# Lightning attention feeding a two-layer MLP on one core: every transpose of k, q and x' moved from the DMA queue to TensorE, and one more group of layer 2 computed as seven block products

## The chip, the cores and the metric

The kernel runs on one core of one Trainium2 chip. The metric is the device time of one execution in microseconds (us). It is given as the median of several executions, and one further view of the work comes from a single execution that the hardware profiler recorded. Engines are called PE (TensorE), DVE (VectorE), ACT (ScalarE), POOL (GpSimd) and SP (SyncE, which here only issues DMAs); PEld is the weight load of TensorE, which the profile lists apart from the matmuls.

## The reference, cut to what matters

Inputs are q, k, v of shape (4 batches, 8 heads, 768 positions, 64), one decay factor per head, a normalization weight of 512 and two weight matrices of 512 x 2048 and 2048 x 512.

```python
for b in range(nb):                       # blocks of 64 positions
    intra = einsum('bhic,bhjc->bhij', qb, kb) * Dmask       # Dmask = lam^(i-j), lower triangle
    intra = einsum('bhij,bhjd->bhid', intra, vb)
    inter = einsum('bhid,bhde->bhie', qb * lam_pow, kv_state)
    out[:, :, sl] = intra + inter
    kv_state = lam_block * kv_state + einsum('bhsd,bhse->bhde', kb * rev_pow, vb)
# x = out, heads side by side: (4, 768, 512)
xn = (x - mean(x)) / sqrt(var(x) + 1e-6) * g_ln
y  = x + relu(xn @ w_ch1) @ w_ch2
```

## The kernel before, in words

The 3072 rows of x are cut into twelve **windows** u of 256 positions of one batch. Each window goes through an attention part and then, as **group** g = u of two tiles of 128 rows, through the MLP.

The attention part of a window loads k, q and v (`load_in`, lines 76 and 80), scales and casts them to bf16 on POOL, DVE or ACT (`in_k_one`, `in_q_one`, `in_v`; lines 231, 236, 242), and needs k and q transposed, so that the head dimension lies on the partitions. The transposed pair is the tile `kqT`. With it the scores (line 279 in the early windows, 370 later) are multiplied on PE, masked on DVE (289, 376), multiplied with v (`av`, lines 436 and 423), and the part that comes from the running state is added (`inter`, line 449). Between the two halves of `inter` stands a fence, `reader` (line 460): a small copy of the PSUM bank, on ACT for most windows, which PE has to wait for. `norm` (lines 475 to 477) takes the row sums on ACT and writes x', the row minus its mean times the weight, as bf16 `xc` on DVE. The reciprocal standard deviation, `rstd_of` (lines 520 to 525), is applied only after layer 2.

x' must be transposed too (`to_xT`, lines 494 to 511), because layer 1 contracts over the 512 features. Layer 1 of a group is eight steps on PE: each is one PSUM bank, filled by eight matmuls with 256 columns (line 547), or, where a chunk is taken tile by tile, by sixteen with 128 columns (line 658), and emptied by ACT with a ReLU into fp16 `hT` (lines 550, 661). Layer 2 has two forms. Groups 0 to 3 use sixteen plain matmuls with 512 columns per tile (line 684, evicted at 708). Groups from `WG = 4` on use a scheme of **seven block products** in place of eight (`product`, line 582; each is eight matmuls with 256 columns): it needs sums of blocks of `hT` (`h_sums`, lines 565 to 567, DVE), sums of blocks of the weights (`w_sums`, lines 809 to 813, DVE, once), and a longer eviction (`evict`, lines 595 to 615, on ACT, POOL and DVE).

The transposes are done in two ways. `transpose_pe` (line 250, copied at 251) serves the first three windows: PE multiplies by an identity, the result lies in PSUM, and ACT or DVE copies it out. From window 3 on, `transpose_dma` (line 257) and `transpose_both` (line 263) let SP issue a DMA transpose from SBUF to SBUF. `to_xT` uses PE and an ACT copy for windows 0 to 4 (lines 510, 511) and a DMA transpose for windows 5 to 11 (line 503).

The order of the work is written out by hand, from line 1043 to the end. `plan` lists the layer steps of all groups, sixteen for each group from 2 on, and `units(n)` emits the next n of them. Between them stand the attention pieces: `s12`, `Y(u)` and `X(u)` interleave window u's scores with window u - 1's output, and loads, casts, transposes and stores each have their place. Every engine takes its own instructions in the emitted order. PSUM has a pool of four banks `mm` (layer 1, layer 2, `kv`, the early scores), two banks `sc` (scores) and one each of `po0` and `po1` (attention output).

Of the kernel before, what the change touches and what calls it, by code (L numbers as in the profile page):

```python
# [8 lines left out]
BF16 = mybir.dt.bfloat16  # L9
# [8 lines left out]
def kernel(  # L18
# [11 lines left out]
    nc = tc.nc  # L30
# [5 lines left out]
    DM = H * D  # L36
    DF = moe_w_ch1.shape[1]
    NP = H // 2
# [5 lines left out]
    XS = 64.0  # L44
    WG = 4
    assert D == 64 and S % W == 0 and DM == 512
# [11 lines left out]
    XB = 3  # L58
    X_PE = (2, 3, 4)
    LB = 6  # L60
# [191 lines left out]

    def transpose_dma(u, a):
        s = st[u]
        if "kqT" not in s:
            s["kqT"] = wk.tile([128, 2, NP, 2, 128], BF16, tag="kqT", bufs=3, name="kqT")
        nc.sync.dma_start_transpose(s["kqT"][:, a].rearrange("p b j t -> p (b j) t"),
                                    s["kq"][:, a].rearrange("p b j e d -> p (b j e d)"))

    def transpose_both(u):  # L260
        s = st[u]
        s["kqT"] = wk.tile([128, 2, NP, 2, 128], BF16, tag="kqT", bufs=3, name="kqT")
        nc.sync.dma_start_transpose(s["kqT"].rearrange("p a b j t -> p (a b j) t"),
                                    s["kq"].rearrange("p a b j e d -> p (a b j e d)"))

# [189 lines left out]
    def reader(u, act=False):  # L455
        s = st[u]
        for ab in range(2):
            if s["S"][ab][1] is not None:
                seen = wk.tile([128, H], F32, tag="seen", name="seen")
                (nc.scalar.copy if act or u > WG else nc.vector.tensor_copy)(seen, s["po"][ab][:, :, 0])  # L460

# [32 lines left out]
    def to_xT(u, ab):  # L494
        s = st[u]
        t = 2 * u + ab
        g = group_of[t]
        i = t - groups[g][0]
        if i == 0:
            xT_of[g] = gp.tile([128, KA, GT * 128], BF16, tag="xT", bufs=3, name="xT")  # L500
        dst = xT_of[g][:, :, i * 128:(i + 1) * 128]
        if u >= 2 and u not in X_PE:
            nc.sync.dma_start_transpose(dst, s["xc"][:, ab])
        else:
            if u < 2:
                xt = mm_tile([128, KA, 128], BF16, "xt")
            else:
                xt = ps.tile([128, KA, 128], BF16, tag=f"po{ab}", name="xt")
            for kk in range(KA):
                nc.tensor.transpose(xt[:, kk, :], s["xc"][:, ab, kk * 128:(kk + 1) * 128], ident)  # L510
            nc.scalar.copy(dst, xt)  # L511

# [19 lines left out]
    def mlp(g):  # L532
# [134 lines left out]
        def m2(i, part):  # L667
# [13 lines left out]
            if part == 0:  # L681
                acc[i] = mm_tile([128, DM], F32, "pm2")
            for kk in range(part * 4, part * 4 + 4):
                nc.tensor.matmul(acc[i], lhsT=hT[:, kk, i * 128:(i + 1) * 128], rhs=w2[kk // W2K][:, kk % W2K, :],  # L684
                                 start=(kk == 0), stop=(kk == KB - 1))
            if part == KB // 4 - 1:
# [251 lines left out]

    def Y(u):
        kv(u)  # L940
        av(u - 1, range(NP))
        inter(u - 1, 0, fence=False)
        reader(u - 1, act=True)
        scores(u, 0)
        scores(u, 1, early=True)
        inter(u - 1, 1)
        new_state(u, 0, nc.gpsimd)
        mask(u, 0, (0,))
        new_state(u, 1, nc.gpsimd)
        norm(u - 1, 0)  # L950
        norm(u - 1, 1)
        mask(u, 1)
        mask(u, 0, (1,))

# [91 lines left out]
    for g in range(2, len(groups)):  # L1046
        m1, m2 = mlp(g)
        lo = {3: 3, 4: 3, 5: 2, 6: 2}.get(g, NWC)
        plan += [(m1, n) for n in range(2 * lo)] + [(m1.tile, c, i) for c in range(lo, NWC) for i in range(2)]
        if g >= WG:  # L1050
            plan += [(m2.w, n) for n in range(8)]
        else:
            plan += [(m2, i, part) for i in range(len(groups[g])) for part in range(KB // 4)]
# [37 lines left out]
    s4(2)  # L1091
    in_k_one(3, nc.vector, 1)
    transpose_dma(3, 0)
    transpose_dma(3, 1)
    load_in(4, "v", nc.sync)
    units(2)
    open_in(5, False)
    load_in(5, "k", nc.sync)
    to_xT(2, 0)
    units(1)  # L1100
    load_in(5, "q", nc.sync)
    rstd_of(2)
# [6 lines left out]
    in_q_one(4, nc.gpsimd, 1)  # L1109
    transpose_dma(4, 0)  # L1110
    transpose_dma(4, 1)
    load_in(5, "v", nc.sync)
# [3 lines left out]
    w_sums(0, 0)  # L1116
    units(2)
    w_sums(0, 1)
    w_sums(1, 0)
    units(3)  # L1120
    s12(3)
    store(0)
    units(3)
    open_window(5)
    in_k_one(5, nc.gpsimd, 0)
    in_k_one(5, nc.gpsimd, 1)
    in_q_one(5, nc.gpsimd, 0)
    in_q_one(5, nc.gpsimd, 1)
    units(2)
    w_sums(1, 1)  # L1130
    open_in(6, False)
    load_in(6, "k", nc.sync)
    units(1)
    load_in(6, "q", nc.sync)
    units(1)
    load_in(6, "v", nc.sync)
    units(1)
    Y(4)
    in_v(5, nc.gpsimd)
    transpose_dma(5, 0)  # L1140
    transpose_dma(5, 1)
    units(3)
    to_xT(3, 0)
    to_xT(3, 1)
    open_in(7, False)
    load_in(7, "k", nc.sync)
    units(1)
    open_window(6)
    in_k_one(6, nc.scalar, 0)
    in_k_one(6, nc.gpsimd, 1)  # L1150
    units(3)
    in_q_one(6, nc.vector, 1)
    in_v(6, nc.gpsimd)
    open_window(7)
    units(1)
    in_q_one(6, nc.vector, 0)
    w_sums(2, 0)
    units(1)
    w_sums(2, 1)
    units(2)  # L1160
    load_in(7, "q", nc.sync)
    w_sums(3, 0)
    units(1)
    rstd_of(3)
    w_sums(3, 1)
    open_in(8, False)
    units(4)
    Y(5)
    transpose_dma(6, 1)
    load_in(7, "v", nc.sync)  # L1170
    units(1)
    in_q_one(7, nc.gpsimd, 0)
    units(1)
    to_xT(4, 0)
    in_q_one(7, nc.gpsimd, 1)
    transpose_dma(6, 0)
    units(1)
    to_xT(4, 1)
    units(1)
    rstd_of(4)  # L1180
    units(2)
    in_k_one(7, nc.vector, 1)
    load_in(8, "k", nc.sync)
    load_in(8, "q", nc.sync)
    in_v(7, nc.gpsimd)
    units(1)
    in_k_one(7, nc.scalar, 0)
    units(1)
    m2s[4].sums(0, 4)
    units(1)  # L1190
    X(6, rest=False)
    open_window(8)
    transpose_dma(7, 0)
    transpose_dma(7, 1)
    to_xT(5, 0)
    to_xT(5, 1)
    store(1)
    store(2)
    units(3)
    m2s[4].sums(4, 8)  # L1200
    mask64(6, 1)
    open_in(9, False)
    units(1)
    units(2)
    in_k_one(8, nc.vector, 1)
    load_in(8, "v", nc.sync)
    load_in(9, "k", nc.sync)
    units(2)
    in_q_one(8, nc.gpsimd, 0)
    in_q_one(8, nc.gpsimd, 1)  # L1210
    in_k_one(8, nc.gpsimd, 0)
    rstd_of(5)
    units(3)
    units(1)
    X(7)
    units(1)
    in_v(8, nc.gpsimd)
    units(1)
    to_xT(6, 0)
    transpose_dma(8, 1)  # L1220
    transpose_dma(8, 0)
    to_xT(6, 1)
    load_in(9, "q", nc.sync)
# [6 lines left out]
    load_in(10, "v", nc.sync)  # L1230
    units(2)
    open_window(9)
    units(1)
    m2s[5].sums(4, 8)
    units(3)
    in_k_one(9, nc.scalar, 0)
    units(1)
    in_k_one(9, nc.scalar, 1)
    units(1)
    rstd_of(6)  # L1240
    X(8)
    in_q_one(9, nc.gpsimd, 0)
    units(1)
    in_q_one(9, nc.gpsimd, 1)
    open_window(10)
    units(3)
    open_in(11, False)
    units(1)
    to_xT(7, 0)
    units(1)  # L1250
    transpose_dma(9, 1)
    transpose_dma(9, 0)
    to_xT(7, 1)
    units(2)
    load_in(10, "q", nc.sync)
    store(3)
    units(2)
    m2s[6].sums(0, 4)
    m2s[6].sums(4, 8)
    units(3)  # L1260
    store(4)
    units(3)
    rstd_of(7)
    units(1)
    in_v(9, nc.gpsimd)
    in_k_one(10, nc.gpsimd, 1)
    in_k_one(10, nc.gpsimd, 0)
    X(9)
    in_v(10, nc.gpsimd)
    in_q_one(10, nc.gpsimd, 0)  # L1270
    units(1)
    transpose_dma(10, 0)
    units(1)
    in_q_one(10, nc.vector, 1)
    units(1)
    to_xT(8, 0)
    units(2)
    to_xT(8, 1)
    units(1)
    transpose_dma(10, 1)  # L1280
    units(3)
    m2s[7].sums(0, 4)
    m2s[7].sums(4, 8)
    units(1)
    load_in(11, "q", nc.sync)
    units(1)
    load_in(11, "k", nc.sync)
    units(2)
    load_in(11, "v", nc.sync)
    units(2)  # L1290
    rstd_of(8)
    units(1)
    X(10)
    units(1)
    to_xT(9, 0)
    to_xT(9, 1)
    open_window(11)
    in_q_one(11, nc.gpsimd, 0)
    in_q_one(11, nc.gpsimd, 1)
    units(1)  # L1300
    in_k_one(11, nc.scalar, 0)
    units(1)
    in_k_one(11, nc.scalar, 1)
    transpose_both(11)
    units(1)
    m2s[8].sums(0, 4)
    units(1)
    in_v(11, nc.gpsimd)
    units(3)
    m2s[8].sums(4, 8)  # L1310
    units(1)
    store(5)
    units(6)
    rstd_of(9)
    units(1)
    X(11)
    units(1)
    to_xT(10, 0)
    to_xT(10, 1)
    units(3)  # L1320
    m2s[9].sums(0, 4)
    units(4)
    m2s[9].sums(4, 8)
    units(7)
    rstd_of(10)
    units(1)
    wind_up(11)
    units(1)
    to_xT(11, 0)
    to_xT(11, 1)  # L1330
    store(6)
# [8 lines left out]
    m2s[10].sums(4, 8)  # L1340
    units(7)
    rstd_of(11)
# [36 lines left out]
```

## Time and profile before

| | |
|---|---|
| median of 7 runs | 207.95 us (206.65 to 208.25) |
| the profiled execution | 206.65 us |
| its span, first to last instruction | 204.9 us |
| PE busy, matmuls | 195.7 us, 96% of the span, x3229 |
| DVE busy | 133.3 us, 65% |
| ACT busy | 122.6 us, 60% |
| POOL busy | 84.7 us, 41% |
| granted TensorE clock, mean | 0.998 |
| DMA transposes issued by SP | 17 for kqT, 14 for xT |

The span is shorter than the execution by 1.75 us; that part lies outside the instructions. In the profile's lines, L250 is line 250 of the kernel. A line of a group gives the engine, the operation, output and input tiles, the shapes, the number of instructions, and then the busy time, the mean duration of one, and the idle time before them. A line of the timeline gives the start, the time covered, the engine and the operation. Matmuls overlap, so the mean duration of one is longer than the distance between two of them; that distance is read from the starts in the timeline.

### The profile page before, as it was taken

How to read it: one execution, taken by the hardware profiler on the slowest of the kernel's cores; microseconds unless marked ns; L12 is line 12 of the kernel's file. 1: busy time of each engine (PE TensorE's matmuls, PEld its weight loads, DVE VectorE, ACT ScalarE, POOL GpSimd, SP SyncE). 2: the span in 40 equal slices, each digit the busy share in tenths (PEclk: the TensorE clock that was granted, in tenths of full speed). 3: DMA queues.
4: the chain of work that ended last, by engine and by line, in shares of the span. 5: the costliest groups of instructions: out<-in, count | busy, mean ns of one | idle time of the engine just before them, and what ended most of it. 6: DMA issues, size and time to landing. Idle time of an engine off the chain costs nothing.

```text
span 204.9 us, 7502 instructions
## 1 busy us (share of the span) xinstructions
PE 195.7 (96%) x3229; PEld 158.9 (78%) x3229; DVE 133.3 (65%) x274; ACT 122.6 (60%) x284; POOL 84.7 (41%) x117
## 2 busy tenths in 40 slices
PE   1998999999999999999999999999999999999992
PEld 0587789544785695588899899888888888988881
DVE  3589351636784764949876774795868947865353
ACT  3788578535352565786485875576586665652730
POOL 5557049117766504533834351872264202002020
PEclk9999999999999999999999999999999999999999
DMA  3999999999899899999999899899979020148404
GB/s 103 301 251 225 187 282 180 194 287 281 174 248 269 192 183 217 183 223 179 156 234 109 179 196 197 184 248 133 217 157 206 4 51 3 28 108 282 153 7 97
DMA packets 91011, 36.41 MB, mean 178 GB/s; under 512 B 65121, under 2 KB 88161, under 8 KB 90978
## 3 DMA queue, kind: packets, MB, share of 16 engines
q1 hardware_dynamic: 86368, 31.53, 74.4%
q0 software_dynamic: 4224, 4.19, 13.0%
q8 instruction: 25, 0.41, 0.9%
q10 hardware_dynamic: 386, 0.20, 0.4%
q14 instruction: 8, 0.07, 0.1%
HBM read 27.27 MB, written 6.29 MB: 164 GB/s over the span
## 4 chain that ended last, share of the span: by engine, by line
PE 82%; DMA 6%; DVE 4%; ACT 4%; issue 1%; POOL 1%; SPq 1%; POOLq 0%; DVEq 0%; ACTq 0%
PE pm L547 33%; PE pm L684 13%; PE pwd L582 6%; PE pwa L582 6%; PE pwc L582 6%; PE pm1t L658 6%; DMA w<-in_moe_w_ch_dram 3%; PE pwb L582 3%; DMA qin<-in_q_dram 3%; PE po L449 1%; PE po L436 1%; DVE x L595 1%; PE po L423 1%; PE pk L324 1%; ACT xT L511 1%
## 5 line engine op out<-in xcount | busy, mean ns | idle before, releaser
L547 PE MATMUL pm<-xT,w 128*128 128x256 bf16 x640 | 73.6, 273 | 0.4 <-DMA w<-in_moe_w_ch_dram 0.4
L547 PEld LDWEIGHTS <-w 128*128 128x128 bf16 x640 | 61.4, 98 | 9.0 <-DMA w<-in_moe_w_ch_dram 0.5
L550 ACT ACTIVATE hT<-pm 128x512 f16<-128x512 f32 x80 | 47.0, 597 | 25.8 <-PE pm L547 25.4
L684 PE MATMUL pm<-w,hT 128*128 128x512 f16 x128 | 29.6, 379 | 0.0
L582 PEld LDWEIGHTS <-hs 128*128 128x128 f16 x256 | 24.9, 98 | 2.9
L565 DVE TENSOR_TENSOR hs<-hT 128x1024 f16<-128x1024 f16 x16 | 12.1, 755 | 18.4 <-ACT hT L550 15.0
L607 POOL TENSOR_TENSOR x<-ev_u,x 128x256 f32<-128x256 f32 x8 | 5.8, 728 | 43.9 <-ACT ev_u L606 32.5
L684 PEld LDWEIGHTS <-hT 128*128 128x128 f16 x128 | 11.8, 98 | 12.6
L330 POOL TENSOR_TENSOR Sn<-Stmp,lam_s 128x256 bf16<-128x256 f32 x16 | 9.9, 622 | 26.8 <-DVE Stmp L408 18.5
L582 PEld LDWEIGHTS <-hT 128*128 128x128 f16 x192 | 18.7, 98 | 2.1
L242 POOL TENSOR_TENSOR vb<-vin,lam_p 128x1024 bf16<-128x1024 f32 x6 | 11.7, 1946 | 11.5 <-DMA vin<-in_v_dram 6.4
L658 PE MATMUL pm1t<-xT,w 128*128 128x128 bf16 x256 | 15.8, 219 | 0.6 <-ACT xT L511 0.3
L658 PEld LDWEIGHTS <-w 128*128 128x128 bf16 x256 | 14.9, 98 | 1.4 <-issue 0.7
L475 ACT ACTIVATE x<-po 128x512 f32<-128x512 f32 x18 | 10.6, 590 | 8.3 <-PE po L449 4.9
L477 DVE SCALAR_TENSOR_TENSOR xc<-po,nmean,g_row 128x512 bf16<-128x512 f32 x18 | 12.9, 744 | 2.6 <-ACT nmean L476 2.5
L520 ACT ACTIVATE sq<-x,nmean 128x512 bf16<-128x512 f32 x18 | 12.9, 718 | 0.3
L242 POOL TENSOR_TENSOR vb<-vin,lam_v 128x1024 bf16<-128x1024 f32 (+1 forms) x7 | 11.6, 1661 | 3.1 <-DMA vin<-in_v_dram 3.0
L661 ACT ACTIVATE hT<-pm1t 128x512 f16<-128x512 f32 x16 | 9.6, 598 | 4.6 <-PE pm1t L658 4.6
L236 POOL TENSOR_TENSOR kq<-qin,lam_p 128x512 bf16<-128x512 f32 x9 | 9.9, 1113 | 1.5 <-DMA qin<-in_q_dram 1.5
L595 DVE SCALAR_TENSOR_TENSOR x<-pwd,rstd,x 128x256 f32<-128x256 f32 x16 | 7.7, 482 | 3.4 <-POOL x L615 3.4
L595 DVE SCALAR_TENSOR_TENSOR x<-pwa,rstd,x 128x512 f32<-128x512 f32 (+1 forms) x16 | 9.1, 613 | 0.7
L582 PE MATMUL pwa<-w,hT 128*128 128x256 f16 x64 | 9.6, 273 | 0.0
(137 smaller groups left out, 321.1 us busy)
## 6 DMA issues: line engine op xcount, KB each, us to landing
out_dram<-x SPq DMA_DIRECT2D x22, 256.0 KB, 4.0
w<-in_moe_w_ch_dram POOLq DMA_DIRECT2D x8, 512.0 KB, 7.9
kin<-in_k_dram SPq DMA_DIRECT2D x14, 256.0 KB, 5.0
qin<-in_q_dram SPq DMA_DIRECT2D x14, 256.0 KB, 4.9
vin<-in_v_dram SPq DMA_DIRECT2D x14, 256.0 KB, 5.2
kin<-in_k_dram SPq DMA_DIRECT2D x5, 512.0 KB, 6.5
qin<-in_q_dram SPq DMA_DIRECT2D x5, 512.0 KB, 7.7
vin<-in_v_dram SPq DMA_DIRECT2D x5, 512.0 KB, 7.2
```

Of the source, the lines that this page charges most:

```text
L236: eng.tensor_tensor(part(1, st[u]["kq"], ALL)[:, :, :, j], src[:, :, :, j], lq[:, :, :, None].to_broadcast([128, NP, 2, D]), op=ALU.mult)
L242: eng.tensor_tensor(st[u]["vb"][:, hs], qkv_in[u]["v"][:, hs], lv.to_broadcast([128, n, 2, D]), op=ALU.mult)
L475: nc.scalar.activation(x, po, ACT.Copy, accum_out=sm)
L477: nc.vector.scalar_tensor_tensor(xc, in0=po, scalar=nm, in1=g_row, op0=ALU.add, op1=ALU.mult)
L520: nc.scalar.activation(sq, s["x"][:, ab], ACT.Square, bias=s["nmean"][:, ab:ab + 1], accum_out=ss[:, ab:ab + 1])
L547: nc.tensor.matmul(pm[:, b, :], lhsT=w1[n // W2K][:, kk, (n % W2K) * 128:(n % W2K + 1) * 128], rhs=xT_of[g][:, kk, 0:N], start=(b == 0 and ...
L550: nc.scalar.activation(hT[:, u * NB:(u + 1) * NB, 0:N], pm, ACT.Relu)
L565: nc.vector.tensor_tensor(s13, b[:, :, 1:2, :].to_broadcast([128, n, 2, 128]), b[:, :, 0:4:3, :], op=ALU.subtract)
L582: nc.tensor.matmul(pr[bank], lhsT=lhs(r), rhs=rhs, start=(first and r == 0), stop=(r == KB // 2 - 1), skip_group_check=True)
L595: nc.vector.scalar_tensor_tensor(out, in0=in0, scalar=r[ab], in1=in1, op0=ALU.mult, op1=ALU.add)
L658: nc.tensor.matmul(pm[:, b, :], lhsT=w1[c][:, kk, b * 128:(b + 1) * 128], rhs=xT_of[g][:, kk, i * 128:(i + 1) * 128], start=(b == 0 and kk ...
L684: nc.tensor.matmul(acc[i], lhsT=hT[:, kk, i * 128:(i + 1) * 128], rhs=w2[kk // W2K][:, kk % W2K, :], start=(kk == 0), stop=(kk == KB - 1))
```

## The change

Three things change, and the hand-written order is set anew around them.

First, `transpose_dma` and `transpose_both` are gone. `transpose_kq(u, a, eng)` takes their place: eight PE transposes (two for each of the four head pairs) of k (a = 0) or of q (a = 1) into one `sc` bank, and one copy of 128 x 1024 bf16 to `kqT`, on ACT sixteen times and on DVE twice. `to_xT` always uses four PE transposes into a `po` bank and an ACT copy. The calls stand mostly among the layer 2 steps.

Second, `WG` becomes 3, so that group 3 takes the seven block products too. All sums of weights therefore come earlier, and `Y(5)` emits the sums of group 3 and reorders its masks.

Third, plan steps change shape: some plain layer 2 steps (all of tiles 3 and 5, the last parts of tiles 1 and 2) are split into two matmuls with 256 columns where there was one with 512, and the chunks of layer 1 that are taken tile by tile are others (eight chunks in groups 2, 5, 6 and 7, where there were six in groups 3 to 6).

```diff
-    WG = 4
+    WG = 3
+    M2_SPLIT = [(t, i) for t in (3, 5) for i in range(4)] + [(1, 3), (2, 3)]
...
-    X_PE = (2, 3, 4)
...
-    def transpose_dma(u, a):
+    def transpose_kq(u, a, eng):
         s = st[u]
         if "kqT" not in s:
             s["kqT"] = wk.tile([128, 2, NP, 2, 128], BF16, tag="kqT", bufs=3, name="kqT")
-        nc.sync.dma_start_transpose(s["kqT"][:, a].rearrange("p b j t -> p (b j) t"),
-                                    s["kq"][:, a].rearrange("p b j e d -> p (b j e d)"))
...
+        tp = ps.tile([128, NP, 2, 128], BF16, tag="sc", bufs=2, name="tp")
+        for p in range(NP):
+            for j in range(2):
+                nc.tensor.transpose(tp[:, p, j, :], s["kq"][:, a, p, j], ident)
+        (eng.copy if eng is nc.scalar else eng.tensor_copy)(s["kqT"][:, a], tp)
...
-        if u >= 2 and u not in X_PE:
-            nc.sync.dma_start_transpose(dst, s["xc"][:, ab])
+        if u < 2:
+            xt = mm_tile([128, KA, 128], BF16, "xt")
         else:
...
+            xt = ps.tile([128, KA, 128], BF16, tag=f"po{ab}", name="xt")
+        for kk in range(KA):
+            nc.tensor.transpose(xt[:, kk, :], s["xc"][:, ab, kk * 128:(kk + 1) * 128], ident)
+        nc.scalar.copy(dst, xt)
...
+            n_z = 2 if (t, part) in M2_SPLIT else 1
             for kk in range(part * 4, part * 4 + 4):
-                nc.tensor.matmul(acc[i], lhsT=hT[:, kk, i * 128:(i + 1) * 128], rhs=w2[kk // W2K][:, kk % W2K, :],
-                                 start=(kk == 0), stop=(kk == KB - 1))
+                for z in range(n_z):
+                    zs = slice(z * DM // n_z, (z + 1) * DM // n_z)
+                    nc.tensor.matmul(acc[i][:, zs], lhsT=hT[:, kk, i * 128:(i + 1) * 128], rhs=w2[kk // W2K][:, kk % W2K, zs],
+                                     start=(kk == 0 and z == 0), stop=(kk == KB - 1), skip_group_check=t in (1, 2, 3, 5))
...
-    def Y(u):
+    def Y(u, sums=None):
...
-        mask(u, 0, (0,))
+        if sums is None:
+            mask(u, 0, (0,))
+        else:
+            mask(u, 1, (0,))
         new_state(u, 1, nc.gpsimd)
+        if sums is not None:
+            mask(u, 1, (1,))
+            m2s[sums].sums(4, 8)
         norm(u - 1, 0)
         norm(u - 1, 1)
-        mask(u, 1)
-        mask(u, 0, (1,))
+        if sums is None:
+            mask(u, 1)
+            mask(u, 0, (1,))
...
-        lo = {3: 3, 4: 3, 5: 2, 6: 2}.get(g, NWC)
-        plan += [(m1, n) for n in range(2 * lo)] + [(m1.tile, c, i) for c in range(lo, NWC) for i in range(2)]
+        tiles = {2: (0, 1, 2), 5: (3,), 6: (2, 3), 7: (1, 2)}.get(g, ())
+        for c in range(NWC):
+            plan += [(m1.tile, c, i) for i in range(2)] if c in tiles else [(m1, 2 * c + i) for i in range(2)]
```

The order around window 6 and around the layer 2 steps of group 6, as it is after the change (the other windows follow the second pattern with shifts). In the first stretch the first step shown is the last layer 2 step of group 3, and the four after it are steps 0 to 3 of group 4's layer 1. The second stretch shows the layer 2 steps 1 to 7 of group 6.

```python
    units(1)
    ...
    units(1)
    in_q_one(7, nc.gpsimd, 0)
    in_q_one(7, nc.gpsimd, 1)
    transpose_kq(6, 0, nc.scalar)
    units(1)
    transpose_kq(6, 1, nc.vector)
    rstd_of(4)
    in_k_one(7, nc.vector, 1)
    in_v(7, nc.gpsimd)
    units(2)
    X(6, rest=False)
    ...
    in_v(9, nc.gpsimd)
    units(1)
    transpose_kq(9, 0, nc.scalar)
    units(1)
    transpose_kq(9, 1, nc.scalar)
    units(1)
    to_xT(7, 0)
    units(1)
    to_xT(7, 1)
    units(2)
    rstd_of(7)
    units(1)
```

## The prediction

> **What bounds the kernel now.** I read the engine totals first, then the slices, then who PE waited for.
>
> ```profile
> PE 195.7 (96%) x3229; PEld 158.9 (78%) x3229; DVE 133.3 (65%) x274; ACT 122.6 (60%) x284; POOL 84.7 (41%) x117
> ...
> PE   1998999999999999999999999999999999999992
> ...
> PEclk9999999999999999999999999999999999999999
> DMA  3999999999899899999999899899979020148404
> ```
>
> PE is busy in every slice but the first and the last, at the full granted clock. The DMA engines look just as busy up to slice 32, so two resources could be the bound. The list of PE's waits tells them apart:
>
> ```profile
> PE g_all L180 <- DMA g_one<-in_moe_g_ln_dram: 4.2, 1, 4.2
> PE pm L547 <- DMA w<-in_moe_w_ch_dram: 0.4, 1, 0.4
> PE pm1t L658 <- ACT xT L511: 0.3, 1, 0.3
> PE pm1t L658 <- DVE Smid L405: 0.2, 1, 0.2
> ```
>
> That is all of it: 5.1 us, of which 4.6 us is startup and waits for weights. PE waits for no transpose and, after the weights, for no load. A crowded DMA queue could still hurt by slowing the matmuls themselves. Two stretches by window exclude that; the columns are length, then busy time and count of PE, PEld, DVE, ACT, POOL, then clock, DMA share and GB/s:
>
> ```profile
> 132.02:139.11 7.09, 7.09 (x66) 6.36 (x67) 6.67 (x11) 5.58 (x13) 4.67 (x5) 1.00 1.05 239
> 160.85:167.98 7.13, 7.13 (x67) 6.38 (x67) 4.97 (x10) 5.63 (x13) 1.36 (x3) 1.00 0.19 39
> ```
>
> Each is the layer 1 of one group, 64 matmuls of line 547. The DMA share falls from 1.05 to 0.19 and the matmuls take the same time, 7.09 and 7.13 us. So the bound is the number of columns that PE has to stream, and DMA relief is worth nothing to it.
>
> **Prices on PE.** "Busy" includes the pipeline's tail, so I take distances between starts. From the timeline (start, time covered, engine, line, operation, count):
>
> ```profile
> 46.07 0.39 PE L510 MATMUL xt<-ident,xc 128*128 128x128 bf16 x4
> 46.29 1.03 PE L684 MATMUL pm<-w,hT 128*128 128x512 f16 x4
> 47.16 0.39 PE L510 MATMUL xt<-ident,xc 128*128 128x128 bf16 x4
> 47.38 5.34 PE L684 MATMUL pm<-w,hT 128*128 128x512 f16 x24
> 52.56 3.66 PE L547 MATMUL pm<-xT,w 128*128 128x256 bf16 x32
> ...
> 75.08 1.95 PE L658 MATMUL pm1t<-xT,w 128*128 128x128 bf16 x32
> 76.87 1.46 PE L684 MATMUL pm<-w,hT 128*128 128x512 f16 x6
> ...
> 183.41 1.04 PE L582 MATMUL pwc<-wt,hs 128*128 128x256 f16 x8
> 184.28 1.04 PE L582 MATMUL pwd<-wt,hs 128*128 128x256 f16 x8
> ```
>
> Four transposes hold the queue from 46.07 to 46.29 and again from 47.16 to 47.38: 0.22 us, 55 to 56 ns each, with nothing lost at the change from 512-column fp16 matmuls and back. The 24 matmuls from 47.38 to 52.56 give 216 ns for 512 columns, the step from 183.41 to 184.28 gives 0.87 / 8 = 109 ns for 256, and 75.08 to 76.87 gives 1.79 / 32 = 56 ns for 128. These prices fit columns alone.
>
> **The change on PE, part by part.** Counts are those of the two programs.
> - Transposes: nine windows x 16 for kqT = 144, and seven x 8 for xT = 56. 200 x 56 ns = **+11.2 us**.
> - Group 3's layer 2: 32 x 216 = 6.91 us go, 56 x 109 = 6.10 us come: **-0.8 us**.
> - Splitting: 40 matmuls of 512 become 80 of 256. No row here shows two halves in one bank. At 109 against 216 it is 40 x 2 ns = 0.08 us; the nearest bounds are 0 (exactly half of 216) and 40 x 6 = 0.24 us (line 547's 7.13 us / 64 = 111 ns). I take **+0.1**, by the block products, fp16 with 256 columns as well.
> - Layer 1: 32 matmuls of 256 become 64 of 128: 3.58 - 3.49 = **+0.1 us**.
>
> The sum is **+10.5 us** of issue time on an engine that has about 0.5 us of late pauses to hide it in.
>
> [...] The row of line 510 has 229 ns as the mean of one, but 56 ns from one start to the next, and the granted clock stays at 1.00 in the slices that hold them. [...]
>
> **What lies beside PE.** ACT gets 16 copies of 128 x 1024 at 1.045 us (the one such copy at line 251) and 14 of 128 x 512 at 0.586 us (line 511), one more pair of evictions at 0.474 us each, and one cast less: 16.7 + 8.2 + 0.9 - 0.6 = +25.3 us, to 148 us of some 217. In a layer 2 stretch (139.11 to 145.23, by window) ACT is busy 3.36 of 6.12 us; it becomes 3.36 + 2 x 1.045 + 2 x 0.586 = 6.62 of 7.46 us, since PE's own 24 transposes lengthen the stretch by 1.34 us. That fits, with little left. DVE gets two copies (0.69 us each) and group 3's sums and evictions, about +6 us on 133: hidden, except as below. SP loses 31 transposes (2.3 us each for 16 of kqT, 1.2 us for xT, in its queue); loads and stores that stood behind them start sooner, and no wait of PE shrinks, since PE waits for none. If the loads were late instead, the casts on POOL and DVE would be, and then the transposes, which now stand in PE's own queue with all later matmuls behind them. The order leaves a dozen or more plan steps of 0.76 to 0.87 us between a window's loads and its transposes, so over 9 us, against 5 us from issue to landing; I cost this at nothing.
>
> **New waits on PE.** The copies lengthen ACT's queue ahead of what PE waits for. I followed the order with the durations above:
> - Window 6 (0 is the end of group 3's layer 2). PE: two layer 1 steps and 16 transposes until 2.65, two more steps until 4.4, then X(6), whose second half of `inter` is due 1.3 us later, at 5.7. It must wait for `reader`, which stands on ACT behind evict 0, the copy of k, evict 1 (until 3.2), `rstd_of(4)` and evicts 2 and 3. The same pieces stood like this before:
>
> ```profile
> 86.06 0.72 ACT L520 ACTIVATE sq<-x,nmean 128x512 bf16<-128x512 f32 x1
> ...
> 87.96 1.70 ACT L550 ACTIVATE hT<-pm 128x512 f16<-128x512 f32 x3
> ...
> 91.61 0.23 ACT L460 COPY seen<-po 128x8 f32<-128x8 f32 x2 [0.20 <-PE po L449]
> ```
>
>   Here `rstd_of(4)` ran from 86.06 to 87.96 and ACT was idle 0.20 us before the reader. Afterwards it runs 3.2 to 5.1, the two evictions until 6.2, the reader until 6.4: PE stands **0.7 us**, and layer 1 waits behind it.
> - Group 3's first layer 2 step needs the two banks of `kv(5)`. The second is freed on DVE after mask, state sum (0.68 + 0.41 us) behind the scores: **0.4 us**. The plain form needed one bank.
> - After X(8), `rstd_of(6)` stands ahead of layer 1's first eviction. From X(8)'s start ACT runs the reader (until 1.25), norm (2 x 0.97), rstd (1.9) and the eviction (0.6), until 5.7. PE, after X (1.2), one layer 2 step (0.76) and four layer 1 steps (3.5), wants that bank at 5.4: **0.3 us**. At X(10) and X(11) `rstd_of` ends about when the reader is due: 0.1 us each. Late evictions of group 4: 0.1 us.
>
> Together 1.7 us, less 0.2 us for the wait of 0.2 us on Smid (94 us) that the new order need not have: **+1.5 us**. These have no row; the ends are 0 (my queue on ACT is too pessimistic) and about 4 us (one exposed copy of 1.045 us at each of four more windows).
>
> **Sum.** 206.65 + 10.5 + 1.5 = 218.65 us against the profiled execution. That one was the fastest of those shown; their median is 1.3 us higher. I can't tell whether that surplus stays without the DMA transposes, so I add half of it: **219.3 us**.
>
> **Rivals.**
> - *All waits hidden* (0.13). PE pays columns alone and the late pauses go: 206.65 + 10.5 - 0.5 = 216.65. For it: ACT has 32% left. Against it: its order in window 6.
> - *ACT becomes a second bound* (0.15). The rstd-before-reader queue recurs at X(7) to X(11), about 0.7 us each, and a copy ahead of the evictions costs as much again in some: +10.5 + 5.5 to 6, so about 223 us. It decides once ACT is over 1 us behind PE at the start of X. For it: 6.62 of 7.46 us in layer 2.
> - *Faster than before* (0.02). The DMA transposes hold PE's pace down, and without them matmuls come closer together. It decides where 12 of some 207 us of issue, 6%, are won, so where a 256-column step falls below 103 ns; at 101 ns (7%) the time would be 218.65 - 15 = about 204 us. The two stretches at 7.09 and 7.13 us speak against it, as does PE's wait list.
> - *The change doesn't take PE's time* (0.01): the transposes fall into pauses and the time stays at 207 to 209. There are not 10 us of pauses.
>
> The forecast itself, columns and one to three us of waits, gets 0.69. The range 216.6 to 222.8 takes in it, the case without waits, and the bound of 4 us on the waits from the median's side (207.95 + 14.5 = 222.45); most of the ACT case is left out. A measurement of this kernel tells about 0.5% from no change. Slower by over 0.5%: 0.97; within: 0.01; faster: 0.02.
>
> **What the profile afterwards would show.** Right: PE's matmul busy time near 206, `tp` at line 250 or its successor with 56 ns between starts, 64 layer 1 matmuls still 7.0 to 7.1 us, DMA share well under 1 with no gain from it, and a wait of PE after the reader's copy near the first X. Wrong: a 256-column step under 107 ns, or PE idle for over 4 us behind ACT copies (ACT case), or waits for `kq` ahead of the transposes (late loads).

## The result and the profile after

The changed kernel takes 219.38 us (median of 20 runs, 218.3 to 221.52) against 207.71 us before (47 runs, 206.56 to 211.35): a ratio of 1.0562, 95% interval 1.054 to 1.0584. The profiled execution took 218.92 us, its span 217.2 us, 12.3 us more than before. The medians of three runs below ("X(8) later", "X(8) and rstd_of(6) later" and the last one) include one slower execution each that their ratios leave out; in the first of them it is the profiled one, whose granted clock fell to 0.5 at 22.3 to 25.7 us, ahead of everything that is read from it here.

The engine totals and slices of the page after the change:

```profile
PE 205.6 (95%) x3525; PEld 175.6 (81%) x3525; DVE 142.0 (65%) x286; ACT 144.3 (66%) x315; POOL 86.4 (40%) x120
...
PE   2977999999999999999999989999999999999992
...
PEclk9999999999999999999999999999999999999998
DMA  4999999999998999949599030030040130310403
```

PE is as full as before and has 9.9 us more to do, while the DMA row falls away from slice 23 on (before, from slice 32 on). Group 9's layer 1, by window with the columns as before, still takes what its columns cost, 64 x 109 ns = 6.98 us:

```profile
172.06:179.04 6.98, 6.98 (x73) 6.28 (x65) 5.04 (x10) 5.60 (x13) 1.36 (x3) 1.00 0.34 77
```

The transposes in layer 2 of group 5, from PE's timeline, cost 116.76 - 116.31 = 0.45 us for eight, 56 ns each, as forecast:

```profile
116.31 0.61 PE L260 MATMUL tp<-ident,kq 128*128 128x128 bf16 x8
116.76 0.27 PE L576 MATMUL pwa<-w,hT 128*128 128x256 f16 x1
...
117.52 0.61 PE L260 MATMUL tp<-ident,kq 128*128 128x128 bf16 x8
117.97 0.27 PE L576 MATMUL pwc<-wt,hs 128*128 128x256 f16 x1
```

The span before the first layer 2 matmul holds the same code in both kernels and took 37.07 and 37.37 us. From that matmul to the start of PE's last one, which I call the **steady stretch**, it is 163.70 us before and 175.53 after. In that stretch the trace has 264 more instructions of 128 columns, 136 more fp16 matmuls of 256, 32 fewer bf16 matmuls of 256 and 72 fewer matmuls of 512. At the forecast's prices that is +10.57 of these +11.83 us; 1.26 us is left. Starts that come over 0.05 us later than is usual at their place add to 2.1 us in the changed kernel and to 0.9 us before, so nearly all of it is waiting. After the last matmul stand 4.2 and 4.3 us. PE's list of waits after the change, in full, has one entry of size that the list before lacks and that is not startup, the second:

```profile
PE g_all L180 <- DMA g_one<-in_moe_g_ln_dram: 4.2, 1, 4.2
PE pm L541 <- DVE x L589: 0.6, 1, 0.6
PE pm1t L652 <- DMA w<-in_moe_w_ch_dram: 0.5, 1, 0.5
PE pm L541 <- DMA w<-in_moe_w_ch_dram: 0.5, 1, 0.5
PE tp L250 <- POOL kq L226: 0.3, 1, 0.3
PE tp L250 <- ACT kq L215: 0.3, 1, 0.3
PE pm1t L652 <- ACT xT L505: 0.2, 1, 0.2
PE po L433 <- DVE vin L783: 0.2, 1, 0.2
```

### The profile page after: what moved, and what is told of

Same layout as the page of the kernel before. It is cut to its first block, busy times and chain, and to the rows that moved or that the text cites. A ratio compares the mean times of both kernels' runs of the same rounds, so it can differ in the third digit from the quotient of the medians.

```text
span 217.2 us, 8079 instructions
## 1 busy us (share of the span) xinstructions
PE 205.6 (95%) x3525; PEld 175.6 (81%) x3525; DVE 142.0 (65%) x286; ACT 144.3 (66%) x315; POOL 86.4 (40%) x120
## 3 DMA queue, kind: packets, MB, share of 16 engines
q1 hardware_dynamic: 59776, 24.97, 48.1%
## 4 chain that ended last, share of the span: by engine, by line
PE 80%; ACT 7%; DMA 5%; DVE 4%; issue 1%; POOL 1%; POOLq 0%; ACTq 0%; DVEq 0%
PE pm L541 28%; PE pm L681 10%; PE pm1t L652 8%; PE pwa L576 6%; PE pwc L576 6%; PE pwd L576 5%; DMA w<-in_moe_w_ch_dram 3%; PE tp L260 3%; PE pwb L576 3%; DVE x L589 3%; PE xt L504 2%; ACT hT L544 2%; PE tp L250 1%; PE po L446 1%; ACT sq L514 1%; DMA g_one<-in_moe_g_ln_dram 1%
## 5 line engine op out<-in xcount | busy, mean ns | idle before, releaser
L541 PE MATMUL pm<-xT,w 128*128 128x256 bf16 x608 | 70.9, 273 | 1.1 <-DVE x L589 0.6
L544 ACT ACTIVATE hT<-pm 128x512 f16<-128x512 f32 x76 | 44.3, 597 | 18.7 <-PE pm L541 18.5
L576 PEld LDWEIGHTS <-hs 128*128 128x128 f16 x288 | 27.2, 98 | 3.0 <-DVE hs L559 0.2
L559 DVE TENSOR_TENSOR hs<-hT 128x1024 f16<-128x1024 f16 x18 | 15.4, 857 | 15.0 <-ACT hT L544 12.7
L261 ACT COPY kqT<-tp 128x1024 bf16<-128x1024 bf16 x16 | 16.2, 1013 | 12.4 <-PE tp L260 12.4
L681 PE MATMUL pm<-w,hT 128*128 128x256 f16 (+1 forms) x136 | 22.7, 317 | 0.0
L576 PEld LDWEIGHTS <-hT 128*128 128x128 f16 x216 | 20.7, 98 | 2.3
L652 PE MATMUL pm1t<-xT,w 128*128 128x128 bf16 x320 | 19.4, 219 | 0.9 <-DMA w<-in_moe_w_ch_dram 0.5
L681 PEld LDWEIGHTS <-hT 128*128 128x128 f16 x136 | 12.7, 98 | 6.0
L505 ACT COPY xT<-xt 128x512 bf16<-128x512 bf16 x24 | 14.0, 589 | 4.7 <-PE xt L504 4.2
L472 ACT ACTIVATE x<-po 128x512 f32<-128x512 f32 x18 | 10.6, 590 | 8.7 <-PE po L446 5.3
L655 ACT ACTIVATE hT<-pm1t 128x512 f16<-128x512 f32 x20 | 11.8, 597 | 6.3 <-PE pm1t L652 6.3
```

The costliest lines, as they stand in the source:

```text
L261: (eng.copy if eng is nc.scalar else eng.tensor_copy)(s["kqT"][:, a], tp)
L541: nc.tensor.matmul(pm[:, b, :], lhsT=w1[n // W2K][:, kk, (n % W2K) * 128:(n % W2K + 1) * 128], rhs=xT_of[g][:, kk, 0:N], start=(b == 0 and ...
L544: nc.scalar.activation(hT[:, u * NB:(u + 1) * NB, 0:N], pm, ACT.Relu)
L559: nc.vector.tensor_tensor(s13, b[:, :, 1:2, :].to_broadcast([128, n, 2, 128]), b[:, :, 0:4:3, :], op=ALU.subtract)
L576: nc.tensor.matmul(pr[bank], lhsT=lhs(r), rhs=rhs, start=(first and r == 0), stop=(r == KB // 2 - 1), skip_group_check=True)
L652: nc.tensor.matmul(pm[:, b, :], lhsT=w1[c][:, kk, b * 128:(b + 1) * 128], rhs=xT_of[g][:, kk, i * 128:(i + 1) * 128], start=(b == 0 and kk ...
```

## The experiments

The theory was that PE's streamed columns set the time; the rivals were ACT's copies, the DMA traffic, and single waits. The first 37 to 41 us vary from one execution to the next with unchanged code, so beside the medians I give the steady stretch of the profiled execution (steady, 163.70 us before, 175.53 after).

| run | median us | ratio to before, 95% interval | steady us |
|---|---|---|---|
| PE transposes of k, q twice | 228.56 | 1.1025 (1.0964 to 1.1086) | 185.65 |
| ACT copies of k, q twice | 230.29 | 1.1079 (1.1018 to 1.1139) | 186.87 |
| DMA transposes beside | 219.03 | 1.055 (1.0503 to 1.0597) | 175.58 |
| no split | 222.35 | 1.0698 (1.0633 to 1.0763) | 177.97 |
| other 40 split | 220.03 | 1.0606 (1.0561 to 1.0651) | 175.47 |
| X(8) later | 219.34 | 1.0561 (1.0519 to 1.0602) | 175.29 |
| X(8) and rstd_of(6) later | 218.96 | 1.0527 (1.0483 to 1.0572) | 174.76 |
| before + x' by PE, DMA's places | 227.62 | 1.0967 (1.0925 to 1.1009) | 183.68 |
| before + x' by PE, layer 2's places | 212.84 | 1.0248 (1.0204 to 1.0293) | 170.10 |
| before + seven products | 209.3 | 1.0089 (1.0056 to 1.0121) | 165.71 |
| before + seven products, moved | 207.29 | 0.9997 (0.9967 to 1.0026) | 163.45 |
| before + seven products, x' of window 2 by DMA | 220.16 | 1.0614 (1.0569 to 1.066) | 176.47 |

**1. Twice the PE transposes.**

```diff
-                nc.tensor.transpose(tp[:, p, j, :], s["kq"][:, a, p, j], ident)
+                for _ in range(2):
+                    nc.tensor.transpose(tp[:, p, j, :], s["kq"][:, a, p, j], ident)
```

> The changed kernel with every PE transpose of k and q issued twice into the same PSUM place: 144 more transposes, not one more copy. Columns theory (PE's streamed columns set the time): 144 x 56 ns = +8.0 us on the 219.4 us of the changed kernel, 227.4 us, ratio to before 1.095; the span grows by the same. Rival, ACT's copies set the time and transposes fill pauses of PE: within 1 us of 219.4.

The median rose by 9.2 us, the steady stretch by 10.1. Of that 8.0 us are the columns (144 x 56 ns); the rest is in PE's waits, under a name that the lists of neither kernel have:

```profile
PE pwc L577 <- issue: 1.5, 1, 1.5
...
PE po L447 <- issue: 0.8, 1, 0.8
```

"issue" means that the profile shows nothing that PE waited for. The columns theory holds, ACT is not what the transposes wait for, and something new has to be explained (4).

**2. Twice the ACT copies.**

```diff
         (eng.copy if eng is nc.scalar else eng.tensor_copy)(s["kqT"][:, a], tp)
+        if eng is nc.scalar:
+            eng.copy(s["kqT"][:, a], tp)
```

> The changed kernel with each of the 16 copies of the transposed k and q on ACT made twice: 16 x 1.01 us = +16.2 us of ACT work, nothing on PE. Columns theory: ACT has 73 us left, but its order is fixed, so single waits of PE appear; +1 to +4 us, 220.5 to 223.5 us. Rival, ACT is already the second bound: +8 to +16 us, 227 us or more.

+10.9 us: the rival's number, not mine. PE's waits say how:

```profile
PE pwc L578 <- ACT ev_p L610: 5.3, 5, 1.1
...
PE pwd L578 <- DVE x L591: 1.5, 5, 0.3
PE po L448 <- ACT seen L459: 1.1, 1, 1.1
...
PE sc L278 <- ACT kqT L263: 0.8, 1, 0.8
```

In each of five groups the sixth product waits 1.1 us for the eviction of the third, `ev_p`, which stands on ACT behind the copies. In the changed kernel itself that wait doesn't occur. So its copies fit, but less than one copy's time is left in front of that eviction: two more copies ahead of it, 2 x 1.01 us, made 1.1 us of wait, so some 0.9 us was free (an estimate). ACT's 34% of idle time is no measure of that slack.

**3. The DMA traffic brought back.**

```diff
+        unread = wk.tile([128, NP, 2, 128], BF16, tag="unread", bufs=2, name="unread")
+        nc.sync.dma_start_transpose(unread.rearrange("p b j t -> p (b j) t"),
+                                    s["kq"][:, a].rearrange("p b j e d -> p (b j e d)"))
```

> The changed kernel, and beside every copy of transposed k or q a DMA transpose of the same half into a tile that nothing reads (18 of them; the pool of the transposed tiles has two buffers in place of three to make room). DMA traffic comes back, PE's work stays. Columns theory: no change, 219.4 us within 0.7, and 256-column matmuls keep 109 ns. Rival, the DMA transposes slow PE or its loads, and their removal has paid back part of the price: 222 us or more, at 3 to 10 us for two thirds of the traffic.

219.03 us and a steady stretch of 175.58, against 219.38 and 175.53, although the main DMA queue moved 29.70 MB again (24.97 in the changed kernel, 31.53 before). By window, layer 2 of group 6 in the changed kernel and in this run:

```profile
131.63:139.08 7.45, 7.45 (x83) 6.82 (x81) 3.69 (x8) 5.80 (x11) 2.57 (x4) 1.00 0.01 2
```

```profile
131.77:139.22 7.45, 7.45 (x83) 6.82 (x81) 3.69 (x8) 5.80 (x11) 2.56 (x4) 1.00 1.06 240
```

The DMA share is 0.01 and 1.06, and both take 7.45 us. So the 18 transposes of k and q cost nothing beside PE's work, and their removal paid back nothing. Those of x' weren't put back.

**4. The split.** The splitting of 40 layer 2 matmuls was taken out:

```diff
-            n_z = 2 if (t, part) in M2_SPLIT else 1
+            n_z = 1
```

> The changed kernel without the splitting of 40 layer 2 matmuls. Columns theory: 40 x 2 ns = -0.1 us, not to be told from 219.4 us. Rival, halves in one bank cost more than their columns: -0.3 us or more, and steps of the halves well over 109 ns in the changed kernel's trace.

3.0 us slower in the median (four executions, 220.74 to 223.22) and 2.4 us in the steady stretch, which neither side of my expectation allowed. PE's timeline inside Y(5):

```profile
82.08 0.34 PE L276 MATMUL sce<-kqT 64*64 64x128 bf16 x10
84.38 0.25 PE L276 MATMUL sce<-kqT 64*64 64x128 bf16 x4 [1.96 <-issue]
```

PE stops in the middle of one group of equal matmuls, for nothing that the program orders. Number PE's matmuls and weight loads by their start, and call each a row: the stop is at row 2752, and the two stops of run 1 are at rows 3008 and 3520. All three are 192 above a multiple of 256. The trace's instruction queue (q8) brings 16 KB at a time, in the changed kernel 27 pieces for 7050 rows, about 63 bytes a row, so about 260 rows a piece; in this run a piece started at 81.7 us and took 1.3 us. Outside the attention parts 256 rows last 14 us (128 matmuls of 109 ns). In an attention part the starts of the matmuls are on average 8 to 11 ns apart (changed kernel, behind the first 20 us), and my reading is that PE outruns its instructions there. So the worth of the split should be its 80 rows, not the halves. The test split 40 other matmuls, all ahead of Y(5):

```diff
-    M2_SPLIT = [(t, i) for t in (3, 5) for i in range(4)] + [(1, 3), (2, 3)]
+    M2_SPLIT = [(0, i) for i in range(4)] + [(t, i) for t in (1, 2) for i in range(3)]
```

> The changed kernel with 40 other layer 2 matmuls split (all of tile 0 and the first three parts of tiles 1 and 2) in place of the 40 that the change splits. Without any split PE stood 1.96 us inside Y(5) for no engine and no load, at its row 2752, and two such stops in the run with doubled transposes were at rows 3008 and 3520: each 192 above a multiple of 256, while its instructions arrive in pieces of 16 KB. Theory, instructions arriving late: the split's worth is its 80 rows, which move the piece boundary out of Y(5), so any 40 splits ahead of it give 219.4 us and no such stop. Rival, these very splits matter (banks, DVE's evictions): 222 us as without any.

The stop is gone and the steady stretch is 175.47 us, the changed kernel's within 0.1 us; the median of 220.03 us has an interval that holds 1.0562. That it is the number of rows ahead of Y(5), and not which matmuls are split, is shown. That PE waits there for a piece of instructions is a reading, and the traces bear it out: each of the 14 has as many pieces as rows of the series 192, 448, 704 and so on. Paired in order, each such row but the first with the piece before it, PE never starts the row sooner than 2.44 us after its piece started (353 pairs), and at the three stops it goes on 2.55, 2.44 and 2.72 us after. My expectation had the 80 rows move the place out of Y(5), and that was wrong: in the changed kernel row 2752 is in Y(5) too, at 80.81 us, without a stop. But there the row before it in the series, 2496, comes at 76.52 us, ahead of Y(5), and the piece for 2752 started at 75.8 us. Without the split 2496 was in Y(5) as well, at 80.87 us, and the piece started only behind it. What decides when a piece is asked for stays open.

**5. The wait of 0.6 us after X(8).** The timelines around it in the changed kernel, DVE's, PE's and ACT's in turn:

```profile
124.75 1.40 DVE L474 SCALAR_TENSOR_TENSOR xc<-po,nmean,g_row 128x512 bf16<-128x512 f32 x2
126.06 0.68 DVE L373 TENSOR_TENSOR mA<-sc,keep 128x512 bf16<-128x512 f32 x1
126.66 0.47 DVE L589 SCALAR_TENSOR_TENSOR x<-pwd,rstd,x 128x256 f32<-128x256 f32 x1
```

```profile
127.19 1.03 PE L541 MATMUL pm<-xT,w 128*128 128x256 bf16 x8 [0.61 <-DVE x L589]
```

```profile
126.51 0.29 ACT L515 ACTIVATE std<-ss,eps_t 128x2 f32<-128x2 f32 x1
126.72 1.55 ACT L544 ACTIVATE hT<-pm 128x512 f16<-128x512 f32 x3
```

The bank that PE wants is the last block product's, and its eviction stands on DVE behind the norm and the mask of X(8). I moved X(8) behind that product:

```diff
-    units(1)
+    units(2)
     X(8)
     in_q_one(9, nc.gpsimd, 0)
-    units(1)
     in_q_one(9, nc.gpsimd, 1)
```

> The changed kernel with X(8) emitted after the last layer 2 step of group 5 in place of ahead of it. In the changed kernel PE stood 0.67 us at 126.3 us for a bank whose eviction stood on DVE behind X(8)'s norm and mask. If that is the cause: -0.6 us, 218.8 us, and the wait is gone from the list. Rival, ACT's rstd ahead of the first eviction is the cause, as the forecast had it: the wait stays.

The wait stayed, with another releaser:

```profile
PE pm1t L652 <- ACT hT L544: 0.7, 1, 0.7
```

Now it is ACT's first eviction behind `rstd_of(6)`, the cause that the forecast had named. Above, both ended within 0.2 us of each other: DVE's at 127.13, ACT's first at about 127.3. So both had to move:

```diff
+    units(2)
     X(8)
...
-    rstd_of(6)
...
     m2s[6].sums(4, 8)
+    rstd_of(6)
```

> The changed kernel with X(8) after the last layer 2 step of group 5 and rstd_of(6) moved from ahead of layer 1 of group 6 to behind its sums. With X(8) alone moved, the wait of 0.65 us stayed and its releaser changed from DVE's eviction to ACT's. Theory, both queues were late by about the same: the wait goes, 218.7 us, layer 1 of group 6 without a step over 0.3 us. Rival, a third cause holds the bank: the wait stays and the time is 219.4 us.

The wait is gone from the list, and the steady stretch is 174.76 us, 0.8 less. The median, 218.96 us, points the same way, but the interval of its ratio, 1.0483 to 1.0572, holds the changed kernel's 1.0562.

**6. x' alone by PE.** First at the places of the DMA transposes:

```diff
-    X_PE = (2, 3, 4)
+    X_PE = tuple(range(2, 12))
```

> The kernel before with x' transposed by PE in all windows, at the places where the DMA transposes were issued, so with the ACT copies in layer 1's stretches; k and q stay on the DMA queue. Columns theory: 56 x 56 ns = +3.1 us of PE issue, and waits for ACT or DVE of up to 2 us because these places were chosen for a DMA: 210.8 to 212.8 us, ratio 1.015 to 1.025. Rival, part of the price is paid back by the free DMA queue: under 210 us.

It cost 20 us, where 56 transposes are 3.1. PE's waits:

```profile
PE xt L510 <- DVE xc L477: 7.8, 7, 3.2
...
PE xt L510 <- DVE xc L884: 3.4, 2, 1.8
```

A DMA transpose that is issued right behind X waits in SP's queue for `xc` (in the kernel before up to 7.7 us for line 477), and PE's list of waits before names none. A PE transpose at the same place holds all later matmuls: 11.2 us in nine waits. The granted clock also fell to 0.5 twice, for 3.4 and 6.8 us; half of these 10.2 us, some 5 us, is an estimate of what that cost (at 0.5 a matmul took 203 ns in run 8 where 109 is usual). With the waits and the 3.1 us of columns that makes 19.4 of the 20 us. Then the same 56 transposes at the changed kernel's places in layer 2:

```diff
+    X_PE = tuple(range(2, 12))
...
-    to_xT(7, 0)
...
-    to_xT(7, 1)
...
     store(4)
-    units(3)
+    to_xT(7, 0)
+    units(1)
+    to_xT(7, 1)
+    units(2)
```

> The kernel before with x' transposed by PE in all windows, this time at the places of the changed kernel, among the layer 2 steps; k and q stay on the DMA queue. Columns theory: 3.1 us of PE issue and hardly a wait, 210.5 to 211.5 us, ratio 1.015 to 1.02, against 227.6 us at the DMA's places; up to 2 us more if a piece of PE's instructions now arrives inside an attention part. Rival, PE transposes of x' cost more than their columns wherever they stand: 214 us or more.

212.84 us, 5.1 above before in place of 20. The steady stretch grew by 6.4 us: 3.1 of columns and two waits:

```profile
PE pm1t L658 <- DVE Smid L405: 1.8, 1, 1.8
...
PE po L449 <- ACT seen L460: 1.1, 1, 1.1
```

The 1.1 us is the reader's, behind the ACT copies, two casts and `rstd_of(6)`. The 1.8 us comes from this pair:

```profile
91.66 2.32 DVE L565 TENSOR_TENSOR hs<-hT 128x1024 f16<-128x1024 f16 x1 [2.10 <-ACT hT L550]
```

```profile
91.54 1.90 POOL L242 TENSOR_TENSOR vb<-vin,lam_p 128x1024 bf16<-128x1024 f32 x1 [3.87 <-DMA vin<-in_v_dram]
```

The first is DVE, the second POOL, both of this run. The sum on DVE took 0.69 us in the kernel before (at 90.70 us, with POOL idle). Here it started 0.1 us after POOL's scaling of v and ended 0.5 us behind it. My upper bound of 211.5 us held neither wait, and the rival's 214 us was not reached.

**7. The seven block products alone,** on the kernel before, with the changed `Y(5)`; the sums of weights stand as early as in the change:

```diff
-    WG = 4
+    WG = 3
...
+    w_sums(2, 0)
+    w_sums(2, 1)
+    w_sums(3, 0)
...
-    Y(5)
+    Y(5, sums=3)
```

> The kernel before with one part of the change alone: group 3's layer 2 as seven block products, with the sums of weights earlier and the masks of window 5 in the changed order; transposes stay on the DMA queue. Columns theory: -0.8 us of PE issue, and no wait for the second bank of the states (the changed kernel showed none where 0.4 us was forecast): 206.9 us, ratio 0.996. Rival, the sums on DVE delay the products or the masks: 207.7 us or more.

```profile
PE po L449 <- ACT seen L460: 1.1, 1, 1.1
PE sce L279 <- DVE x L708: 0.9, 1, 0.9
```

209.3 us: the steady stretch grew by 2.0 us where it should have shrunk by 0.8. Most of the difference is two waits that the changed kernel doesn't have: for the reader behind `rstd_of(3)` on ACT, and for a bank whose eviction stands behind the sums of weights on DVE. I moved both:

```diff
-    w_sums(3, 0)
...
-    units(3)
+    units(2)
+    rstd_of(3)
+    units(1)
     to_xT(3, 0)
...
+    w_sums(3, 0)
     w_sums(3, 1)
...
-    rstd_of(3)
```

> The kernel before with group 3's seven block products, as in the first try, but with the last two weight sums behind Y(4) and rstd_of(3) ahead of the transposes of window 3's x', because the first try stood 0.9 us for a bank behind the weight sums on DVE and 1.1 us for the reader behind rstd_of(3) on ACT. Columns theory: -0.8 us of PE issue and those 2 us gone, 206.9 us, ratio 0.996, faster than both kernels. Rival, new waits of the same size elsewhere: 208 us or more.

207.29 us, ratio 0.9997: not to be told from before. The steady stretch is 0.25 us shorter; of the 0.8 us of columns, 0.3 us is still the wait for that bank, and for the rest I have no single row. So on the kernel before, part two of the change is worth some tenths at most, and no version that I tried is faster than it beyond the noise.

**8. Fewer PE transposes than before.** Run 7's first form, with x' of window 2 by DMA too:

```diff
-    X_PE = (2, 3, 4)
+    X_PE = (3, 4)
```

> The kernel before with group 3's seven block products and with x' of window 2 transposed by DMA too, so 8 PE transposes fewer: the other way round from the change. Columns theory: -0.8 and 8 x 56 ns = -0.4 us, 206.5 us, ratio 0.994, faster than both kernels if the transposed tile lands in time (some 5 us of layer 2 steps lie between). Rival, it lands late and layer 1 of group 2 waits: 207.5 us or more.

The rival won, by far more than its price:

```profile
PE pm L547 <- DMA xT<-xc: 9.7, 1, 9.7
```

SP's queue reached the two transposes at 53.6 and 57.1 us, behind loads and transposes for later windows, and PE stood from 51.9 to 61.9 us. By window (columns as before; the third number from the right is the granted clock):

```profile
51.90:61.80 9.90, 0.26 (x2) 0.00 (x0) 3.76 (x6) 0.00 (x0) 5.37 (x5) 0.62 1.07 244
61.86:64.50 2.64, 2.64 (x13) 1.91 (x14) 0.00 (x0) 0.60 (x1) 0.00 (x0) 0.50 0.90 209
64.60:69.00 4.40, 4.40 (x98) 3.77 (x96) 1.52 (x3) 2.11 (x4) 0.00 (x0) 1.00 1.18 310
```

## Why the prediction was right

**The bound.** That PE's columns set the time, and that an empty DMA queue is worth nothing, is shown twice over: twice the transposes cost their 8.0 us of columns and two stops, and bringing the DMA transposes of k and q back cost 0.05 us of the steady stretch.

**The prices.** 56, 109 and 216 ns held in the changed kernel; priced that way the steady stretch grows by 10.6 us, the forecast's number (its terms add to 10.6, not 10.5). The mean duration of one transpose is 229 ns at line 510 before and 219 ns at line 260 after, while the distance stayed 56 ns. Behind the start, the most transposes in a row are 16 in 0.9 us (run 1), and there the granted clock was 1.00. ACT's busy time came to 144.3 us where 148 was forecast.

**The waits.** +1.5 us were forecast and 1.3 us came. That the sums are so close is luck, since the single waits were not where or as long as I put them:
- X(6), 0.7 us forecast: 0.27 us (the second half of `inter` started 277 ns after the last matmul of the scores, at most 9 ns in every other window). The reader did stand behind `rstd_of(4)` and two evictions on ACT, as the rows show, ACT's first and PE's behind them. PE reached the place where I had it, 5.75 us after layer 1 of group 4 began (forecast 5.7). But the reader let it go on at 6.0 us (94.60) and not at 6.4: I had added ACT's durations, while in the rows an instruction starts some 0.1 us before the one ahead of it ends (93.43 against 93.23 + 0.29).

```profile
93.23 0.29 ACT L515 ACTIVATE std<-ss,eps_t 128x2 f32<-128x2 f32 x1
93.43 1.06 ACT L544 ACTIVATE hT<-pm 128x512 f16<-128x512 f32 x2
94.39 0.23 ACT L457 COPY seen<-po 128x8 f32<-128x8 f32 x2
```

```profile
94.60 0.38 PE L446 MATMUL po<-Sn,kqT 64*64 64x64 bf16 x16
```

- Group 3's second bank, 0.4 us forecast: nothing. PE went from Y(5) into the products at 81.62 with no more than the usual 0.1 us.
- After X(8), 0.3 us forecast behind ACT: 0.6 us by the list (0.8 between starts), and DVE was late as well as ACT (5).
- X(10) and X(11), 0.1 us each: nothing. In their place X(7) lost 0.3 us, a step of layer 1 behind it 0.2, and X(8) itself 0.3, which I had not seen.

**The split** was forecast at +0.1 us by its columns, and as such that is right: 80 halves at 109 ns. But without it the time would have been 222.35 us, near the upper end of the range, for a cause that I had not thought of. The forecast's point came out at 219.3 against 219.38 partly because the change happened to carry 80 rows, with which PE didn't stop in Y(5). That is luck too.

**ACT** was "32% left" in the forecast. Twice the copies showed that the slack in front of one eviction is under one copy, so the ACT case was nearer than its chance of 0.15 made it look.

**The half of 1.3 us** between profiled execution and median: over 47 runs the surplus of before is 1.1 us, over 20 runs that of the changed kernel 0.5 us. Half was about right, but for no reason that I can show.

## What to carry to other kernels

Where two resources look full side by side, as PE and the DMA queue do here, compare two stretches with the same matmuls and different traffic: the one whose times don't change with the other is the bound. Here that told it before any run, and run 3 confirmed it (7.45 us at DMA shares of 0.01 and 1.06). The transposes that moved from a queue that nobody waited for into the bound engine cost their full issue time there (with the rest of the change +10.57 of the +11.83 us), and each wait of theirs became a wait of everything behind it, so their place mattered more than their length (20 or 5 us for the same 56 transposes). Slack was what was left in front of the one instruction that the bound engine waited for (some 0.9 us, the estimate of run 2), not the idle share of an engine (34% for ACT).

## What the runs showed of the hardware that I had not expected

- **Stops that no engine ended.** PE stopped 1.5, 0.8 and 1.96 us at rows 3008, 3520 and 2752, all 192 above a multiple of 256, each time in or just behind an attention part. Such a row never started sooner than 2.44 us after the piece of instructions that I pair with it, in 14 traces. Eighty more rows ahead took the stop at 2752 away.
- **The clock after a pause.** In run 8 PE stood from 51.9 us; the granted clock fell to 0.5 at 54.3 and came back at 64.6, 2.7 us after the work did, and meanwhile 13 matmuls took 2.64 us, 203 ns each where 109 is usual. The spans at 0.5 inside the runs last 3.4, 6.8 or 10.2 us.
- **DVE beside POOL.** The fp16 sum of 128 x 1024 took 0.69 us alone. Where it started during a POOL multiplication it took 0.7 to 2.3 us and ended 0.55 us after POOL did, in all 58 such cases of the 14 traces.
- **The start.** The code ahead of the first layer 2 matmul is the same in both kernels, and it took between 36.9 and 40.6 us in the profiled executions, with PE's listed waits for the first weights between none and 1.8 us. Most of the spread of the runs may be that; I did not test it.
